# A convolution by transforms on one core: the first group of transformed weights made from one copy of the weights, the second copy loaded later, and the other groups cut anew

## The chip, the core and the metric

The kernel runs on one NeuronCore of a Trainium2 chip. The core has TensorE (matrix products, PE in the profile, with PEld for the loading of its stationary operand), VectorE (DVE), ScalarE (ACT), GpSimd (POOL) and SyncE (SP), which issues nearly all transfers, and 16 DMA engines. TensorE writes to eight banks of PSUM; DVE or ACT then copy ("cast") a bank into SBUF. The metric is device microseconds for one execution. The kernel before takes 269.83 us, the median of three runs (269.64 to 270.08).

## The reference

One image of 224 x 224 pixels with 96 channels is convolved with 7 x 7 taps from 96 to 96 channels. The reference does it by real Fourier transforms; only the product over channels mixes them. The convolution wraps round at the edges, since the transforms have the image's size.

```python
# x: (1, 224, 224, 96) bf16, w: (7, 7, 96, 96) bf16
wp = jnp.pad(w, ((0, H - K), (0, W - K), (0, 0), (0, 0)))
Xf = rfft2(x.astype(jnp.float32), axes=(1, 2))
Wf = rfft2(wp.astype(jnp.float32), axes=(0, 1))
Yf = jnp.einsum('bhwi,hwio->bhwo', Xf, Wf)
y = irfft2(Yf, s=(H, W), axes=(1, 2)).astype(jnp.bfloat16)
```

## The kernel before

The kernel does not transform the whole image. Down the image it takes eight blocks of 28 rows, each with a border of six, so 34 rows, and transforms these 34 rows into 17 real-pair "frequencies" (`NS = 17`; the first and the last, `REAL`, are two real numbers each, the other 15 a real and an imaginary part). Across the image it works on tiles of 32 pixels, seven of them (`NT = 7`), even and odd pixels being two planes, and treats the seven taps across by sums of shifted planes: 10 combinations of taps (`NTAP`, `TAPS`) in place of 14.

**The weights.** For each frequency the weights are needed transformed along the seven taps down, and combined along the seven taps across. The result is `WF` (96 input channels in partitions; 50 slots, 10 tap combinations, 96 output channels). A frequency has three slots: real part, imaginary part and their difference (two slots for frequency 0). WF is made on TensorE: the stationary operand is a strided view of the raw weights `wqx` (line 154; taps in partitions, 96 input channels by 96 output channels along each), the moving operand the selection matrix `Em` (line 157), which holds sine and cosine values times tap masks and lies behind the weights in the same buffer. The raw weights lie there twice: partition 2k + h holds tap k from output channel 48 h on, so that one product gives output channel o from the first copy and o + 48 from the second (half h of Em is zero in the partitions of the other). This is 98 partitions. Lines 182 to 187 load them in five chunks of columns, each as two transfers (tap 48 alone, then taps 0 to 47). Lines 188 and 189 let the second half of the first tile's pixels, `load_x(0, 1)`, wait for the third chunk.

`prep_jobs(gi)` (line 340) gives the jobs that make one group of frequencies. A job takes a bank, fills it with four products and has it cast to WF. The groups are `PGRP` (line 33). Group 0 (frequencies 0 and 1) is "full": all three slots come from products, 100 columns each, 12 jobs. The other five groups, three frequencies each, make two slots by products of 120 columns (12 jobs), and DVE subtracts one from the other for the third slot (`diff`, three jobs or two).

**The order of the work.** The calls are written in program order, and each engine runs its own in that order. At the start (lines 178 to 288) SP issues: the halo pixels (six pixels left of the first tile, two buffers `xh_bufs`), the first half of the first tile's pixels, the weight chunks, and the second half. All these pixel buffers lie in the last eight slots of WF, which are written late. TensorE runs 17 products of zeros (`warm`, line 195: filler), while DVE, ACT and POOL build the transform matrix `Fm` and Em from index arithmetic. Lines 699 to 717 then set TensorE's order: pixel transforms of the halos (`a_bank`) and of the first half (`f_jobs`, three parts by frequency, ten banks), 22 fillers, group 0 of the weights, the second half's first part, and then the planes `J` of the first three frequencies (`jit`, on DVE).

**The rounds.** `b_round(t, s)` (line 496) does one tile at one frequency: 33 products of WF with pixel planes in two banks (22 for a REAL frequency), sums on ACT, DVE and POOL, and every three frequencies a transfer to a scratch in DRAM. Frequency 0 of tile 0 is round 0. The first two tiles run interleaved, tile 1 four rounds behind (`LAG`). At two points of a round queued jobs may be run, counted by a slot number k: slots 2r and 2r + 1 belong to round r. A queue entry (a, b, jobs) runs its jobs evenly from slot a to slot b - 1 (`pace`, line 725). Lines 744 and 745 queue the weight groups so: group 1 in slots 0 and 1, group 2 in 4 to 8, and so on to slot 26. The rest of tile 0's pixel transforms and those of tiles 1 and 2 are queued there as well. The later tiles follow from line 808, with the inverse transforms (`c_jobs`), and a tail from line 846.

`evac` (line 120) decides whether DVE or ACT casts a bank: it adds up planned costs, 180 + n for DVE and 160 + 0.85 n for ACT with n columns, and takes the engine whose sum stays lower. The sums start at zero and are set anew before the rounds (line 721). When the last weight group is done, at round 15, the buffer of the raw weights is given back and later stages' pools open in its place (lines 778 to 788).

## Time and profile before

| what | value |
|---|---|
| median of three runs | 269.83 us |
| profiled execution: span from first to last instruction | 267.8 us |
| profiled execution: own time | the page gives its span alone; the median of the runs is 2.0 us above that span |
| PE busy | 258.4 us, 5144 products |
| DVE, ACT, POOL busy | 214.3, 194.6, 98.9 us |
| granted TensorE clock | 1.00 |
| moved by DMA | 46.78 MB, mean 175 GB/s |

The span is cut at the first and the last instruction, so it is a little shorter than the time of an execution. A group's line in the profile names the engine, the operation, what is written from what, the shapes and the count; in the timeline the first two numbers are the start and the length of a run of like instructions, in microseconds. In the table of stages each line has a stretch of time, its length, and then for PE, PEld, DVE, ACT and POOL the busy time and in brackets the number of instructions; at the end stand the granted clock, the DMA engines' busy share and the GB/s they moved. All work goes through helpers, so the source line of every instruction is that of one helper, and groups are told apart by tile names: wq is the buffer of the raw weights with Em, WF the transformed weights and also the early pixel buffers in it, xf the transformed pixels, J their planes, wu the zeros of the filler products, pb a PSUM bank.

### The profile page before, as it was taken

Reading aid. Unit: us, or ns where it says so; the run is one execution under the profiler, and the core shown is the slowest. Engines: PE = TensorE matmul, PEld = TensorE weight load, DVE = VectorE, ACT = ScalarE, POOL = GpSimd, SP = SyncE. Lnnn points to the kernel's source line nnn. Section 1 sums busy time; section 2 is a strip of 40 time slices with the busy share of each in tenths; the row PEclk is TensorE's granted clock in tenths of the full one; section 3 lists DMA queues with packets and bytes.
Section 4 is the critical chain, followed back from the end, with each engine's and each line's share of the span. In section 5 each row is a group of like instructions: output and inputs, shape, how many; then the busy total and the mean of one; then the engine's idle time right before and its main releaser. Section 6 shows DMA issues by size and latency. Waiting matters only on the chain. (4 is left out here: it accounts for less than half of the span.)

```text
span 267.8 us, 12172 instructions
## 1 busy us (share of the span) xinstructions
PE 258.4 (96%) x5144; PEld 237.3 (89%) x5144; DVE 214.3 (80%) x457; ACT 194.6 (73%) x483; POOL 98.9 (37%) x156
## 2 busy tenths in 40 slices
PE   8999999999999999999999999999999999999983
PEld 3679999999999999999999998999999889879862
DVE  5658998889899788779787888787898889878624
ACT  5558988587974577988988789887887854278113
POOL 7782315363656435321422222223222342532100
PEclk9999999999999999999999999999999999999999
DMA  6948011811111498997968487979777624887956
GB/s 169 233 130 213 11 47 46 239 48 72 47 47 50 146 266 143 281 272 199 299 170 241 116 221 235 238 204 329 269 148 216 202 98 154 198 229 186 257 115 206
DMA packets 47014, 46.78 MB, mean 175 GB/s; under 512 B 35286, under 2 KB 37986, under 8 KB 46960
## 3 DMA queue, kind: packets, MB, share of 16 engines
q1 hardware_dynamic: 44672, 43.94, 59.3%
q10 hardware_dynamic: 2288, 2.06, 2.6%
q8 instruction: 40, 0.66, 1.0%
q14 instruction: 14, 0.11, 0.2%
HBM read 24.65 MB, written 21.33 MB: 172 GB/s over the span
## 5 line engine op out<-in xcount | busy, mean ns | idle before, releaser
L89 PE MATMUL pb<-WF,J 96*128 96x96 bf16 x2821 | 162.8, 206 | 1.9 <-DVE J L89 1.1
L89 PEld LDWEIGHTS <-J 96*128 96x128 bf16 x2821 | 138.0, 98 | 12.4 <-issue 3.6
L89 POOL TENSOR_TENSOR yf<-v,u 128x384 bf16<-128x384 f32 x79 | 81.4, 1042 | 146.3 <-issue 84.6
L89 ACT CAST xf<-pb 96x408 bf16<-96x408 f32 (+3 forms) x145 | 67.7, 490 | 9.0 <-PE pb L89 5.4
L89 PE MATMUL pb<-WF,xf 96*128 96x96 bf16 x952 | 59.9, 206 | 0.5 <-ACT xf L89 0.5
L89 DVE TENSOR_TENSOR J<-xf 96x1824 bf16<-96x1824 bf16 (+1 forms) x84 | 56.9, 716 | 0.1
L89 PEld LDWEIGHTS <-xf 96*128 96x128 bf16 x952 | 47.0, 98 | 0.7 <-ACT xf L89 0.6
L89 PE MATMUL pb<-Fm,xn 118*128 118x136 bf16 (+3 forms) x640 | 45.5, 199 | 0.2 <-DVE u L89 0.2
L89 PE MATMUL pb<-tt,Gm 102*84 102x384 bf16 (+1 forms) x132 | 32.7, 326 | 0.4 <-ACT J L89 0.3
L89 ACT CAST WF<-pb 96x480 bf16<-96x480 f32 (+1 forms) x59 | 29.1, 578 | 4.8 <-PE pb L89 4.8
L89 PEld LDWEIGHTS <-xn 118*128 118x128 bf16 x640 | 30.3, 97 | 0.3 <-issue 0.3
L89 ACT CAST J<-pb 84x384 bf16<-84x384 f32 (+1 forms) x64 | 27.7, 490 | 2.6 <-PE pb L89 2.6
L89 ACT CAST yo<-pb 84x384 bf16<-84x384 f32 (+1 forms) x63 | 27.1, 486 | 2.3 <-POOL yf L89 1.3
L89 DVE TENSOR_TENSOR J<-J 96x912 bf16<-96x912 bf16 (+2 forms) x42 | 24.2, 577 | 0.0
L89 PE MATMUL pb<-wq 98*128 98x120 bf16 (+1 forms) x288 | 21.3, 226 | 0.0
L89 PEld LDWEIGHTS <-wq 98*128 98x128 bf16 x288 | 19.6, 151 | 0.2 <-issue 0.2
L89 PE MATMUL pb<-wu 128*128 128x512 bf16 (+1 forms) x75 | 16.8, 385 | 1.1 <-DVE ct L89 1.1
L89 PEld LDWEIGHTS <-wu 128*128 128x128 bf16 (+1 forms) x75 | 8.8, 120 | 8.0 <-issue 2.8
L89 DVE TENSOR_TENSOR yf<-v,u 128x384 bf16<-128x384 f32 x26 | 14.9, 572 | 0.9
L89 PEld LDWEIGHTS <-Gm 102*84 102x84 bf16 (+1 forms) x132 | 11.1, 117 | 1.0 <-issue 0.4
L89 ACT COPY xf<-xf 96x816 bf16<-96x816 bf16 (+3 forms) x20 | 11.3, 633 | 0.0
L89 DVE CAST WF<-pb 96x480 bf16<-96x480 f32 (+1 forms) x13 | 7.5, 609 | 4.2 <-PE pb L89 4.2
(386 smaller groups left out, 234.2 us busy)
## 6 DMA issues: line engine op xcount, KB each, us to landing
scr<-yf SPq DMA_DIRECT2D x30, 288.0 KB
xn<-in_x_dram SPq DMA_DIRECT2D x12, 672.0 KB
tt<-scr SPq DMA_DIRECT2D x24, 336.0 KB
out_dram<-yo SPq DMA_DIRECT2D x12, 252.0 KB
out_dram<-J SPq DMA_DIRECT2D x12, 252.0 KB
tt<-scr SPq DMA_DIRECT2D x6, 288.0 KB
WF<-in_x_dram SPq DMA_DIRECT2D x2, 672.0 KB
out_dram<-tt SPq DMA_DIRECT2D x8, 168.0 KB
```

The costliest lines, as they stand in the source:

```text
L89: r = fn(*a, **k)
```

## The change

The raw weights lie in another order: partition 49 h + k holds tap k from output channel 48 h on. So partitions 0 to 48 are one complete copy (all 96 x 96 columns), partitions 49 to 97 the second copy, shifted by 48 output channels. `load_w(h)` loads one copy in three transfers: tap 48 in two pieces of 16 short runs each, and taps 0 to 47 in one transfer of 48 rows. SP's order becomes: first half of the first tile's pixels, first copy, halos, second half of the pixels, second copy; the wait of the second half for a weight chunk is gone. Em starts 48 columns later, and its index arithmetic follows the new order: two operations more on DVE (`hf`, `tap`), four fewer on POOL, and POOL's clearing of the early pixel buffers' ends stands before the masks in place of behind them.

Group 0 is now four frequencies, made by `wide_jobs`: 24 jobs of four products each (96 products), over the 49 rows of the first copy with half 0 of Em, 110 columns, all slots at once. The other groups have 3, 3, 3 and 4 frequencies and still use both copies; the last one's banks hold 3 products of 160 columns, 16 jobs. Their slots are set by `PWIN`: 0 to 6, 7 to 11, 12 to 16 and 17 to 23.

TensorE's order at the start becomes: 16 fillers, the first half's pixel transforms, 4 fillers (`FILL`), 16 wide jobs (`WMID`), the halos, the second half's first part, the other 8 wide jobs. The raw weights' buffer is given back at round 14.

```diff
--- before.py
+++ after.py
@@ -25,12 +25,13 @@
 TW = 16
 HALO = 3
 PXC = 16
-NB = 8
+NB0 = 4
 POS = TW + HALO
 NTAP = 10
 TAPS = ((7, 8, 9, 6), (0, 2, 4, 6), (1, 3, 5))
 NSLOT = 2 + 3 * (NS - 1)
-PGRP = ((0, 2), (2, 5), (5, 8), (8, 11), (11, 14), (14, 17))
+PGRP = ((0, 4), (4, 7), (7, 10), (10, 13), (13, 17))
+PWIN = (None, (0, 7), (7, 12), (12, 17), (17, 24))
 YGRP = ((0, 3), (3, 6), (6, 9), (9, 12), (12, 15), (15, 17))
 YGRPL = ((0, 3), (3, 6), (6, 9), (9, 12), (12, 15), (15, 17))
 SA = 9
@@ -44,8 +45,8 @@
 MERGE = ()
 NP2 = 0
 WARM = 36
-NWC = 5
-HOLD = 2
+FILL = 4
+WMID = 16
 BIAS = 3000.0
 
 
@@ -152,9 +153,9 @@
     stmp_cm = tc.tile_pool(name="stmp", bufs=1)
     stmp = stmp_cm.__enter__()
     wqx = wtmp.tile([128, C - 1 + 127 * C + 1], BF16, name="wq")
-    wq = wqx[0:PW2]
     WC = C * C - C2
-    Em = wqx[0:PW2, WC:WC + 2 * NSLOT * NTAP].rearrange("p (h a t) -> p h a t", h=2, a=NSLOT)
+    WE = C * C
+    Em = wqx[0:PW2, WE:WE + 2 * NSLOT * NTAP].rearrange("p (h a t) -> p h a t", h=2, a=NSLOT)
     XHW = PAD * C + 32
     late = WF[0:R, NSLOT - 8:NSLOT].rearrange("p a t o -> p (a t o)")
     x0_bufs = [late[:, i * (XW + 32):(i + 1) * (XW + 32)] for i in range(2)]
@@ -176,17 +177,22 @@
         return load_rows(xbuf(t, jg), jg, t * 2 * TW, 2 * TW)
 
     wsrc = w.rearrange("kh kw i o -> (kh kw) (i o)")
+
+    def load_w(h):
+        n = (C * C, WC)[h]
+        off = wsrc.offset + h * C2
+        p = h * PW
+        m = n // 16
+        for a, b in ((0, m // 2), (m // 2, m)):
+            dma(wqx[p + PW - 1:p + PW, 0:n].rearrange("p (c m) -> p c m", c=16)[:, :, a:b],
+                bass.AP(wsrc.tensor, off + (PW - 1) * C * C + a, [[C * C, 1], [m, 16], [1, b - a]]))
+        dma(wqx[p:p + PW - 1, 0:n], bass.AP(wsrc.tensor, off, [[C * C, PW - 1], [1, n]]))
+    load_x(0, 0)
+    load_w(0)
     for jg in range(2):
         load_rows(xh_bufs[jg], jg, W - PAD, PAD)
-    load_x(0, 0)
-    wcut = [WC * c // NWC // 128 * 128 for c in range(NWC)] + [WC]
-    wdma = []
-    for c0, c1 in zip(wcut, wcut[1:]):
-        for k, n in ((PW - 1, 1), (0, PW - 1)):
-            wdma.append(dma(wqx[2 * k:2 * (k + n), c0:c1],
-                bass.AP(wsrc.tensor, wsrc.offset + k * C * C + c0, [[C * C, n], [C2, 2], [1, c1 - c0]])))
-    for d in load_x(0, 1):
-        tc.add_manual_dep(d.ins, wdma[2 * HOLD + 1].ins.name, SYNC, reason="second pixels behind the weights")
+    load_x(0, 1)
+    load_w(1)
 
     wu = cpool.tile([128, 128], BF16, name="wu")
     wur = wu[:].unsqueeze(1).to_broadcast([128, 4, 128])
@@ -197,7 +203,7 @@
         for _ in range(n):
             TE.matmul(pwu[:].rearrange("p (a b) -> p a b", a=4), lhsT=wu[:, 0:128], rhs=wur, start=True, stop=True)
     warm(8)
-    warm(9)
+    warm(8)
 
     ntmp = [0]
 
@@ -217,7 +223,7 @@
     VE.memset(pi_t[:], math.pi)
     dmy = ftile([128, 1])
     SE.activation(out=dmy[:], in_=pi_t[:], func=ACTF.Sin, bias=0.0, scale=0.0)
-    zw = wqx[0:PW2, WC + 2 * NSLOT * NTAP:]
+    zw = wqx[0:PW2, WE + 2 * NSLOT * NTAP:]
     SE.copy(out=zw, in_=wu[0:PW2, 0:1].to_broadcast(list(zw.shape)))
 
     nrj = ftile([R, JG]); pw_i = ftile([R, 1]); aa = ftile([R, NS, 2]); phf = ftile([R, NS, 2]); phe = ftile([R, NS, 2])
@@ -234,7 +240,10 @@
         eng.tensor_scalar(out=out_ap, in0=out_ap, scalar1=MAGIC, scalar2=MAGIC, op0=ALU.add, op1=ALU.subtract)
 
     VE.tensor_scalar(out=nrj[:], in0=nrj[:], scalar1=0.0, scalar2=float(LC - 1), op0=ALU.max, op1=ALU.min)
-    floor_div(VE, thp[:], pw_i[:], 2 * KT)
+    hf = ftile([R, 1]); tap = ftile([R, 1])
+    VE.tensor_single_scalar(out=hf[:], in_=pw_i[:], scalar=float(PW), op=ALU.is_ge)
+    VE.scalar_tensor_tensor(out=tap[:], in0=hf[:], scalar=-float(PW), in1=pw_i[:], op0=ALU.mult, op1=ALU.add)
+    floor_div(VE, thp[:], tap[:], KT)
     VE.memset(aa[:, 0, 1:2], float(LC))
     VE.memset(aa[:, NS - 1, :], 0.0)
     VE.memset(phf[:, 0:NS:NS - 1, 1:2], LC / 2.0)
@@ -253,21 +262,20 @@
     for r, n, v in ((0, 0, 1.0), (0, LC, -1.0), (1, 1, -1.0), (1, L - 1, 1.0)):
         o = mf[:, :, 2 * NS - 2 + r:2 * NS - 1 + r]
         GE.affine_select(out=o, in_=o, pattern=[[-B, JG], [0, 1]], compare_op=ALU.not_equal, fill=v, base=-n, channel_multiplier=1)
+    for xb in x0_bufs:
+        GE.memset(xb[:, XW:], 0.0)
+    for xb in xh_bufs:
+        GE.memset(xb[:, PAD * C:], 0.0)
     iota(twc[:], [[1, KT]])
-    pm = ftile([PW2, 1]); twp = ftile([PW2, 1]); hf = ftile([PW2, 1]); mk = ftile([PW2, NTAP]); mk2 = ftile([PW2, 2, NTAP])
-    th14 = ftile([PW2, 1])
-    GE.tensor_single_scalar(out=th14[:], in_=thp[0:PW2], scalar=-2.0 * KT, op=ALU.mult)
-    GE.tensor_tensor(out=pm[:], in0=th14[:], in1=pw_i[0:PW2], op=ALU.add)
-    floor_div(GE, twp[:], pm[:], 2)
-    GE.tensor_single_scalar(out=th14[:], in_=twp[:], scalar=-2.0, op=ALU.mult)
-    GE.tensor_tensor(out=hf[:], in0=th14[:], in1=pm[:], op=ALU.add)
+    twp = ftile([PW2, 1]); mk = ftile([PW2, NTAP]); mk2 = ftile([PW2, 2, NTAP])
+    th7 = ftile([PW2, 1])
+    GE.tensor_single_scalar(out=th7[:], in_=thp[0:PW2], scalar=-float(KT), op=ALU.mult)
+    GE.tensor_tensor(out=twp[:], in0=th7[:], in1=tap[0:PW2], op=ALU.add)
     GE.tensor_scalar(out=mk[:, 0:KT], in0=twc[:], scalar1=twp[:, 0:1], scalar2=None, op0=ALU.is_equal)
     GE.tensor_tensor(out=mk[:, KT:NTAP], in0=mk[:, 0:6:2], in1=mk[:, 1:6:2], op=ALU.add)
-    GE.tensor_scalar(out=mk2[:, 1], in0=mk[:], scalar1=hf[:, 0:1], scalar2=None, op0=ALU.mult)
+    GE.tensor_scalar(out=mk2[:, 1], in0=mk[:], scalar1=hf[0:PW2, 0:1], scalar2=None, op0=ALU.mult)
     GE.tensor_tensor(out=mk2[:, 0], in0=mk[:], in1=mk2[:, 1], op=ALU.subtract)
-    for xb in xh_bufs:
-        GE.memset(xb[:, PAD * C:], 0.0)
-    for xb in x0_bufs + xn_bufs:
+    for xb in xn_bufs:
         GE.memset(xb[:, XW:], 0.0)
     for xb in xf_bufs:
         GE.memset(xb[:, :, :, NS - 1, POS - 1, :].rearrange("c p r j -> c (p r) j"), 0.0)
@@ -337,31 +345,46 @@
 
     g_fin = build_g(3)
 
+    def wide_jobs():
+        n = slot(PGRP[0][1] - 1, 2) + 1
+        ncol = n * NTAP
+        assert NB0 * ncol <= 512 and C % NB0 == 0
+
+        def mk_(ob):
+            def f():
+                pw = bank()
+                pv_ = pw[:, 0:NB0 * ncol].rearrange("p (k q) -> p k q", q=ncol)
+                ev = Em[0:PW, 0, 0:n, :].rearrange("p a t -> p (a t)")
+                o0 = ob * NB0
+                for k in range(NB0):
+                    o = o0 + k
+                    TE.matmul(pv_[:, k], lhsT=wqx[0:PW, o:o + 127 * C + 1:C], rhs=ev, start=True, stop=True)
+                wv = WF[0:C, 0:n].rearrange("i a t o -> i (a t) o")
+                apart(("W", 0), ob, evac(wv[..., o0:o0 + NB0], pv_[0:C].rearrange("i k q -> i q k"), NB0 * ncol))
+            return f
+        return [mk_(ob) for ob in range(C // NB0)]
+
     def prep_jobs(gi):
         s0, s1 = PGRP[gi]
         ns = s1 - s0
-        full = gi == 0
-        ncol = (NSLOT_OF(s0, s1) if full else 2 * ns) * NTAP
+        ncol = 2 * ns * NTAP
+        hb = 256 // ncol
+        NB = 2 * hb
         nb = C // NB
-        hb = NB // 2
-        assert NB * ncol <= 512 and C2 % hb == 0
+        assert C2 % hb == 0
 
         def mk_(ob):
             def f():
                 pw = bank()
                 pv_ = pw[:, 0:NB * ncol].rearrange("p (k h q) -> p k h q", h=2, q=ncol)
                 ev = Em[:, :, slot(s0, 0):slot(s1 - 1, 2) + 1, :]
-                ev = ev.rearrange("p h a t -> p h (a t)") if full else ev.rearrange("p h (s r) t -> p h s (r t)", r=3)[:, :, :, 0:2 * NTAP]
+                ev = ev.rearrange("p h (s r) t -> p h s (r t)", r=3)[:, :, :, 0:2 * NTAP]
                 for k in range(hb):
                     o = ob * hb + k
                     TE.matmul(pv_[:, k], lhsT=wqx[0:PW2, o:o + 127 * C + 1:C], rhs=ev, start=True, stop=True)
                 pv_ = pv_[0:C]
                 o0, o1 = ob * hb, (ob + 1) * hb
                 wv = WF[0:C, slot(s0, 0):slot(s1 - 1, 2) + 1]
-                if full:
-                    wv = wv.rearrange("i a t (h o) -> i (a t) h o", h=2)
-                    apart(("W", gi), ob, evac(wv[..., o0:o1], pv_.rearrange("i k h q -> i q h k"), NB * ncol))
-                    return
                 wv = wv.rearrange("i (s r) t (h o) -> i s (r t) h o", r=3, h=2)
                 apart(("W", gi), ob, evac(wv[:, :, 0:2 * NTAP, :, o0:o1],
                       pv_.rearrange("i k h (s q) -> i s q h k", s=ns), NB * ncol))
@@ -373,10 +396,7 @@
                 w0, w1, w2 = (WF[0:C, slot(s, r)].rearrange("i t o -> i (t o)") for r in range(3))
                 VE.tensor_tensor(out=w2, in0=w0, in1=w1, op=ALU.subtract)
             return f
-        return [mk_(ob) for ob in range(nb)] + ([] if full else [diff(s) for s in range(s0, s1) if s not in REAL])
-
-    def NSLOT_OF(s0, s1):
-        return slot(s1 - 1, 2) + 1 - slot(s0, 0)
+        return [mk_(ob) for ob in range(nb)] + [diff(s) for s in range(s0, s1) if s not in REAL]
 
     xf_tiles = {}
 
@@ -697,18 +717,20 @@
         pump()
 
     xf0 = new_xf(0)
-    for jg in range(2):
-        for f in a_bank(0, xf0, xh_bufs[jg], 0, 3, jg, 0):
-            f()
     fj = [f_jobs(0, p) for p in range(3)]
     for p in range(3):
         for f in fj[p][0]:
             f()
-    for n in (11, 11):
-        warm(n)
-    for f in prep_jobs(0):
+    warm(FILL)
+    wide = wide_jobs()
+    for f in wide[:WMID]:
         f()
+    for jg in range(2):
+        for f in a_bank(0, xf0, xh_bufs[jg], 0, 3, jg, 0):
+            f()
     last = [f() for f in fj[0][1]]
+    for f in wide[WMID:]:
+        f()
     for jg in range(2):
         for d in load_x(1, jg):
             tc.add_manual_dep(d.ins, last[0].ins.name, SYNC, reason="second tile's pixels later")
@@ -742,7 +764,7 @@
         qs.append([a, b, jobs, len(jobs)])
 
     for gi in range(1, len(PGRP)):
-        add(2 * PGRP[gi - 1][0], 2 * PGRP[gi - 1][1] - (2 if gi == 1 else 1), prep_jobs(gi))
+        add(*PWIN[gi], prep_jobs(gi))
     for t in range(2):
         scr_tiles[t] = dr_pool.tile([TW, NJ, NS, 4 * C], BF16, name="scr")
     bursts = {}
```

## The prediction

> **What bounds the kernel now.** I read the page's shares of busy time first, then busy time by stage.
>
> ```profile
> PE 258.4 (96%) x5144; PEld 237.3 (89%) x5144; DVE 214.3 (80%) x457; ACT 194.6 (73%) x483; POOL 98.9 (37%) x156
> ```
> ```profile
> 10.96:15.71 4.75, 4.75 (x30) 2.19 (x26) 1.14 (x3) 0.58 (x1) 3.52 (x18) 1.00 0.97 255
> 15.71:20.23 4.52, 4.06 (x81) 3.94 (x80) 3.92 (x8) 3.76 (x8) 3.89 (x12) 1.00 0.19 54
> 20.23:35.67 15.44, 15.30 (x362) 15.16 (x363) 14.18 (x27) 14.62 (x36) 3.68 (x5) 1.00 0.43 116
> 80.00:236.00 156.00, 154.40 (x3174) 144.85 (x3172) 130.78 (x279) 119.74 (x308) 53.39 (x56) 1.00 0.73 202
> ```
> From 20.23 us on TensorE is the bound: 154.40 of 156 us busy between 80 and 236, 15.30 of 15.44 in the first rounds. There it is closely followed: DVE 14.18 and ACT 14.62 of 15.44. Before 20.23 a busy TensorE means little, as the order of its work shows:
>
> ```profile
> 1.05 5.83 PE L89 MATMUL pb<-wu 128*128 128x512 bf16 x17 [1.05 <-DVE ct L89]
> 7.62 3.49 PE L89 MATMUL pb<-Fm,WF 118*128 118x136 bf16 x103 [0.44 <-POOL WF L89]
> 10.96 4.91 PE L89 MATMUL pb<-wu 128*128 128x512 bf16 x22
> 15.71 3.13 PE L89 MATMUL pb<-wq 98*128 98x100 bf16 x48
> 18.68 1.10 PE L89 MATMUL pb<-Fm,WF 118*128 118x64 bf16 x32
> 20.23 0.51 PE L89 MATMUL pb<-WF,xf 96*128 96x96 bf16 x8 [0.46 <-ACT xf L89]
> 20.58 2.17 PE L89 MATMUL pb<-wq 98*128 98x120 bf16 x32
> 22.59 0.76 PE L89 MATMUL pb<-WF,J 96*128 96x96 bf16 x14
> 29.51 0.93 PE L89 MATMUL pb<-wq 98*128 98x120 bf16 x12
> ```
> The wu products are filler: 22 of them cover the wait for the weights. Round 0 starts at 20.23, and what follows is nearly all useful. So the time after is: when round 0 starts, plus what TensorE still has to do then. The casts that empty the banks, and the transfers, are the other views:
>
> ```profile
> 16.14 2.09 DVE L89 CAST WF<-pb 96x400 bf16<-96x400 f32 x4 [4.04 <-PE pb L89]
> 20.75 1.51 DVE L89 TENSOR_TENSOR J<-xf 96x1824 bf16<-96x1824 bf16 x2
> 16.40 2.78 ACT L89 CAST WF<-pb 96x400 bf16<-96x400 f32 x6 [4.61 <-PE pb L89]
> ```
> ```profile
> 3.11 7.20 SPq L89 DMA_DIRECT2D wq<-in_w_dram  x10
> 12.93 0.79 SPq L89 DMA_DIRECT2D WF<-in_x_dram  x2
> ```
> ```profile
> 5.00:6.00 1.00, 1.00 (x6) 0.41 (x5) 0.77 (x7) 0.00 (x0) 0.69 (x4) 1.00 1.02 294
> 8.00:9.00 1.00, 0.98 (x30) 0.83 (x28) 1.00 (x2) 0.81 (x2) 0.89 (x2) 1.00 1.02 229
> 12.00:13.00 1.00, 1.00 (x6) 0.49 (x5) 0.10 (x1) 0.00 (x0) 0.74 (x4) 1.00 1.04 246
> ```
>
> **The change part by part.** *Transfers.* In 1000-byte kB: one pixel load 118 x 6144 B = 725, a halo pair 272, first copy 49 x 18432 = 903, second 898. The GB/s of the one-microsecond windows (0, 21, 150, 187, 289, 294, 246, 226, 229, 240, 240, 248, 246 from 0 on) sum to 725 at 5.3 us, 1628 (pixels and first copy) at 8.9, 2625 (halos and second pixels too) at 13.0; at 245 GB/s on from there all 3523 have moved at 16.7. From moved to seen: SP waited until 12.93 for the third of five chunks, whose bytes (272 + 725 + 3/5 of 1797 = 2075) were through at 10.8, so 2.1 us. The first copy is then seen at 11.0, second pixels at 15.1, second copy at 18.8. The curve of before starts with short halo rows (150 and 187); with the pixels' 289 to 294 from 2 us on, all is 0.5 us sooner: 10.5. I take 10.8. SP's issuing is no limit: at 0.38 us a pixel load (2.26 for 6) and 0.72 a weight load, the first copy's three are out at 3.7 and the last at 8.2. Four issues fewer and the lost wait at 12.93 are worth nothing by themselves.
>
> *Constants.* POOL loses four small operations of its mask chain (about 1.1 us of 4.34 to 7.50) and does four memsets (0.31) before it: masks at 6.7 in place of 7.5. DVE gets two one-column operations (0.2 us each): Fm ready at 5.8 in place of 5.4, covered by the 16 filler products that end near 6.5. The selection matrix Em keeps its 1000 columns (1.4 us): 6.7 to 8.1, ahead of DVE's first pixel cast.
>
> *Start of TensorE.* First pixels, moved at 4.5 to 5.3, are seen between 6.6 and 7.4; 96 products at 32 ns (3.49 us for 103 wider ones) take 3.0; four fillers 0.86 (22 in 4.75). The wide group starts near 10.9, as the copy arrives.
>
> *Wide group, halos, second pixels.* 96 products, at 63 ns each (twelve from 29.51 to 30.27), are 6.05 us; with halos (0.7) and second pixels (1.1) 7.85. The trace has none with 49 rows: half of 63 is the lower end and 63 the upper, and I take 63; the casts decide either way. A cast of 400 columns cost DVE 0.523 (2.09/4) and ACT 0.463, single ones of 480 are 0.08 longer on either, so 440 cost 0.56 and 0.50. With four halo casts and four of 512 (DVE 0.53 and 0.62, ACT 0.47 and 0.53), all on DVE would be 18.0 us, all on ACT 15.9; the planner's costs give DVE 45%: 8.1 and 8.7 us. The slower queue decides: start 10.9, 0.43 to the first cast (15.71 to 16.14), 8.7 of casts, 0.1: round 0 at 20.1, against 20.23. If the casts were free, TensorE's 7.85 and 0.6 for the last bank would give 19.4; ten per cent dearer casts give 21.0. So fillers saved (19 x 0.216 = 4.1 us) go into making twice the frequencies, and the start moves by only -0.1.
>
> *Rounds.* TensorE has 240 weight products behind 20.23 before and 144 + 48 after: 48 x 63 = 3.04 less. The last group's 48 run 160 columns: 0.416 ns a column by the fillers (512 in 216, less a fixed 3) gives 69 against 63: +0.28. Net -2.76. There are 52 weight casts in place of 60 and 12 differences in place of 14: (8 x 0.57 + 2 x 0.60)/2 = 2.9 us less for the pair of engines. So the relief is nearly the same whether TensorE or the pair sets the pace. Round 0's fill falls from eight jobs to three (0.76 us); J's first operation (1.1 us) starts as DVE's last wide cast ends, near 19.5, done by 20.7 when it is wanted: no stall, and one of 0.5 at most if DVE runs late. The first fill needs the second copy at 20.5, seen at 18.8; each microsecond beyond that holds round 0's J products, queued behind it, by as much. Second pixels are wanted at 15.8 and seen at 15.1. From round 4 on the weight jobs are denser (37 in 17 slots, 36 in 20), but the pair's demand there, about 34 us, stays under TensorE's 37: nothing, +0.5 if it binds in places. The pools of the later stages open a round sooner, behind the last weight job: nothing. Second tile's loads, two microseconds sooner, run after the second copy: nothing.
>
> *Sum.* -0.1 - 2.76 = -2.9 us. The profiled span of 267.8 would be 264.9. The page gives no other time for that execution; the median of the runs, 269.83, is 2.0 above its span, which I carry over: **266.9 us**.
>
> **Rivals.**
>
> *First copy late (slower).* It lands in 49 partitions by rows of 18 KB, which this trace has nowhere: the time is 266.9 plus its delay behind 10.9, so no gain is left if it is seen at 13.8. Rates of a busy queue bound it: 294 GB/s (pixels), and 118 in the slice from 247 to 247.5 us with a DMA share of 1.01, where the tail's reloads go mostly into 64 partitions. At 118 it takes 7.7 us from 5.3, is seen at 15.1, and the time is 271.1. Against it: those reloads move pieces of 384 B, while long pixel rows got 289 to 294. [...]
>
> *The wide group waits for both copies (the change doesn't do what it says).* Both lie in one buffer; if the wait is kept for the whole buffer, the group starts at 18.8: 7.9 us later, 274.8. What speaks for it is that the kernel itself has to declare parts of a buffer independent for the casts (apart). Against it: pixel products ran at 7.62 while the other pixel buffer of the same WF was filled only after 12.93. [...]
>
> *Copy moderately late*, seen at 12.2 to 13.3: 268.2 to 269.3.
>
> *More than the sum.* The copy seen at 10.2 and casts 5% cheaper give -1.1, fewer stalls in the crowded first rounds up to -0.4: 265.4.
>
> **How the numbers follow.** The forecast, with its own range of 265.4 to 268.2 (start -0.8 to +1.3, rounds -0.7), has 0.70. Moderately late 0.11; no measurable change, 269.3 to 270.4 (seen 13.3 to 14.4), 0.05; later than that 0.08; the wait for both 0.06. This gives faster 0.81, same 0.05, slower 0.14, with 0.2% (0.54 us) as what a measurement here can tell from nothing. The range 265.4 to 269.3 holds 0.81.
>
> **What the profile after would show.** Wide products (49 rows, 110 columns) starting near 10.9 after four fillers, with little idle time and casts back to back on both engines until 20; second copy still arriving to 16.7. Round 0 (first product of WF with xf) near 20.1; 12 weight products and not 32 between it and the first J products; round 0 to round 4 shorter by about 2.3 us. Wrong if the 49-row products wait for DMA beyond 13.8, if round 0 starts past 22.9, or if TensorE idles over 2 us more between 20 and 80.

## The result

The kernel after takes 280.64 us (median of four runs, 278.67 to 284.09), the kernel before 269.95 beside it (269.64 to 270.12). The ratio of the two is 1.0376, with a 95% interval from 1.0308 to 1.0443: slower by 10.7 us, where 2.9 us less were forecast. The profiled execution took 278.85 us, with a span of 276.8 against 267.8. In the four runs the granted clock's mean was 0.975, 0.957, 0.954 and 0.975, and the two with the lower clock are the two long ones (282.44 and 284.09, of which the ratio leaves out the second).

The page's shares of busy time and the row of the granted clock, kernel after:

```profile
PE 259.8 (94%) x5125; PEld 241.2 (87%) x5125; DVE 217.4 (79%) x460; ACT 201.5 (73%) x484; POOL 97.7 (35%) x152
...
PEclk9957999997999999999999999999999999999999
```

There are 19 products fewer, yet PE's busy time rose by 1.4 us, and the clock's row, which was full before, has dips in slices 3 and 4 (13.8 to 27.7 us), and again in slice 10 (62 to 69). The order of TensorE's work in the kernel after:

```profile
6.31 2.69 PE L90 MATMUL pb<-Fm,WF 118*128 118x64 bf16 x96 [0.18 <-DMA WF<-in_x_dram]
8.84 1.02 PE L90 MATMUL pb<-wu 128*128 128x512 bf16 x4
12.76 5.33 PE L90 MATMUL pb<-wq 49*128 49x110 bf16 x64 [2.90 <-DMA wq<-in_w_dram]
18.02 3.22 PE L90 MATMUL pb<-Fm,WF 118*128 118x136 bf16 x44
21.18 2.15 PE L90 MATMUL pb<-wq 49*128 49x110 bf16 x32
24.06 0.50 PE L90 MATMUL pb<-WF,xf 96*128 96x96 bf16 x8 [0.73 <-ACT WF L90]
24.39 1.34 PE L90 MATMUL pb<-wq 98*128 98x120 bf16 x12
...
61.54 0.50 PE L90 MATMUL pb<-WF,xf 96*128 96x96 bf16 x8
63.83 0.47 PE L90 MATMUL pb<-WF,J 96*128 96x96 bf16 x7 [1.79 <-DVE J L90]
```

The first copy is seen at 12.76 after a wait of 2.90 us; round 0 begins at 24.06 and not at 20.1; at 62 TensorE waits 1.79 us for VectorE's planes. The casts of the wide group stood as priced on ACT (five in 2.49 us, 0.50 each). DVE's seven took 0.70 each and not 0.56, since they came at the pace of TensorE's half clock; at full clock (the kernel with 17 fillers and runs of 2, below) seven took 3.96 us, 0.57 each:

```profile
13.23 2.49 ACT L90 CAST WF<-pb 96x440 bf16<-96x440 f32 x5 [3.95 <-PE pb L90]
13.48 4.89 DVE L90 CAST WF<-pb 96x440 bf16<-96x440 f32 x7 [2.87 <-PE pb L90]
```

To see where the time came in, I line the traces up by the start of the same product of WF with xf (there are 952, eight to a round), and take its time after less its time before:

| product | before, us | after, us | difference |
|---|---|---|---|
| 0 (round 0) | 20.23 | 24.06 | +3.83 |
| 48 | 38.98 | 43.82 | +4.84 |
| 112 | 57.23 | 61.54 | +4.31 |
| 144 | 65.97 | 74.12 | +8.15 |
| 224 | 85.05 | 93.69 | +8.63 |
| 951 (last) | 250.38 | 259.07 | +8.69 |

So 3.83 us come in before round 0, about 0.5 from there to product 112, 4.3 between products 112 and 224 (where the last group of weights is made), and nothing behind. The stretches between those products in the table of stages (length, then busy time of PE, PEld, DVE, ACT and POOL), before:

```profile
20.23:57.23 37.00, 36.66 (x869) 36.38 (x869) 34.05 (x65) 30.61 (x76) 12.08 (x13) 1.00 0.38 105
57.23:85.05 27.82, 27.27 (x638) 26.98 (x636) 24.03 (x48) 21.09 (x51) 16.20 (x17) 1.00 0.15 56
20.23:85.05 64.82, 63.92 (x1502) 63.36 (x1503) 58.08 (x111) 51.70 (x125) 28.28 (x29) 1.00 0.28 84
```

and after; the last line lies 9 us behind 80 to 236 of the kernel before, and its shares are nearly the same (154.35 of 156 us for TensorE, where it had 154.40):

```profile
14.30:21.10 6.80, 6.80 (x86) 6.65 (x84) 5.38 (x9) 5.16 (x11) 4.58 (x13) 0.50 0.64 158
24.06:61.54 37.48, 36.95 (x854) 36.81 (x853) 32.02 (x59) 30.74 (x73) 11.91 (x11) 0.95 0.29 86
61.54:93.69 32.15, 27.59 (x606) 27.02 (x604) 25.59 (x50) 23.14 (x45) 15.61 (x16) 0.95 0.13 49
89.00:245.00 156.00, 154.35 (x3175) 144.84 (x3173) 129.18 (x276) 120.66 (x311) 53.20 (x55) 1.00 0.73 203
```

In the rounds TensorE's idle time (length less busy) went from 0.90 us to 5.08, and its busy time rose by 0.63 (from 63.92 to 36.95 + 27.59) although 48 weight products are gone from them. The granted clock stands at 0.50 from 14.3 to 21.1, 24.5 to 27.9 and 65.5 to 68.9: stretches of 3.4 us or two of them.

### The profile page after: what moved, and what is told of

It reads as the page before. It is cut to its first block, busy times and chain, and to the rows that moved or that the text cites. A ratio compares the mean times of both kernels' runs of the same rounds, so it can differ in the third digit from the quotient of the medians.

```text
span 276.8 us, 12123 instructions
## 1 busy us (share of the span) xinstructions
PE 259.8 (94%) x5125; PEld 241.2 (87%) x5125; DVE 217.4 (79%) x460; ACT 201.5 (73%) x484; POOL 97.7 (35%) x152
## 4 chain that ended last, share of the span: by engine, by line
PE 73%; DMA 10%; DVE 9%; ACT 4%; issue 2%; SPq 1%; ACTq 0%; DVEq 0%
PE pb L90 73%; DMA wq<-in_w_dram 3%; DVE J L90 3%; DMA xf<-scra 2%; DMA tt<-scr 2%; DVE v L90 2%; DVE WF L90 2%; ACT WF L90 2%; SPq L90 1%; DMA scrb<-yf 1%; DMA xf<-scrb 1%; DVE u L90 1%; ACT J L90 1%; DVE yf L90 1%; ACT xf L90 1%
## 5 line engine op out<-in xcount | busy, mean ns | idle before, releaser
L90 DVE TENSOR_TENSOR J<-xf 96x1824 bf16<-96x1824 bf16 (+1 forms) x84 | 56.2, 709 | 0.0
L90 ACT CAST WF<-pb 96x480 bf16<-96x480 f32 (+1 forms) x59 | 35.1, 666 | 6.8 <-PE pb L90 6.7
L90 PE MATMUL pb<-wq 98*128 98x120 bf16 (+2 forms) x288 | 24.9, 245 | 2.9 <-DMA wq<-in_w_dram 2.9
L90 PEld LDWEIGHTS <-wq 98*128 98x128 bf16 (+1 forms) x288 | 22.2, 152 | 3.4 <-issue 3.4
L90 DVE CAST WF<-pb 96x440 bf16<-96x440 f32 (+1 forms) x17 | 11.0, 657 | 3.6 <-PE pb L90 2.9
L90 PE MATMUL pb<-wu 128*112 128x384 bf16 (+1 forms) x56 | 12.1, 376 | 1.1 <-DVE ct L90 1.1
L90 PEld LDWEIGHTS <-wu 128*112 128x112 bf16 (+1 forms) x56 | 6.8, 124 | 5.5 <-issue 2.2
```

Of the source, the lines that this page charges most:

```text
L90: r = fn(*a, **k)
```

## The experiments

Six theories were tested. **A**: idle time ahead of the wide group halves the clock. **B**: the last group's casts, whose innermost runs in WF are three elements long instead of four, are dear. **C**: the first copy is late since its partitions are only part of all. **D**: a group's differences, three in a row on VectorE ahead of the planes J, make TensorE wait. **E**: products over 49 rows leave TensorE too little active, and this halves the clock. **F**: VectorE is as full as TensorE in the rounds, so that fewer products alone bring little.

**Fillers up to the copy (A).** `FILL` goes from 4 to 17; in a second kernel the last group also takes two products a bank (runs of 2), and a third has that group's change alone.

```diff
-FILL = 4
+FILL = 17
```

> The changed kernel with 17 fillers in place of 4 between the first pixels and the first copy (13 more of 0.216 us, 2.8 us, so TensorE has work while it waits). Theory A (TensorE's idle 2.9 us before the first copy halved its clock from 14.3 to 21.1 us and, after the next gap, from 24.5 to 27.9): no half clock before 60 us, the first copy still seen near 12.7, round 0 at 12.8 + 0.43 + 8.7 + 0.1 = 22.0 in place of 24.06, time 3 to 4 us below the changed kernel, 275 to 277. The loss between 57 and 87 us stays. Rival (the casts set that stage's pace, the clock doesn't matter): round 0 stays near 24, time within 0.5 us of the changed kernel.

277.72 us, ratio 1.0256 (1.0219 to 1.0293). In its profile TensorE has no gap ahead of the wide group, and yet the clock is halved for 13.7 us:

```profile
9.72 3.83 PE L90 MATMUL pb<-wu 128*128 128x512 bf16 x17
13.49 4.56 PE L90 MATMUL pb<-wq 49*128 49x110 bf16 x64
```
```profile
16.70:30.40 13.70, 13.09 (x161) 12.73 (x160) 8.32 (x14) 10.17 (x23) 3.03 (x8) 0.50 0.49 133
```

So a gap is not needed, and A as stated falls, although the time fell by about the 3 us that A forecast (by the two ratios 3.2). The mean clock was 0.969 in this profile and 0.980 to 0.988 in the other three executions, so none ran at full clock throughout.

```diff
-        hb = 256 // ncol
+        hb = min(256 // ncol, 4 if ns == 3 else 2)
```

> The changed kernel with the last group's banks holding 2 products of 160 columns (24 casts of 320 columns, runs of 2 output channels) in place of 3 (16 casts of 480, runs of 3). Theory B (a cast that writes runs of three 2-byte values costs 0.9 us on ScalarE and 1.2 on VectorE, and these 16 casts hold up TensorE from 57 to 87 us): casts of 320 at 0.38 to 0.48, the distance to the kernel before grows by less than 1.5 us between 57 and 87 us in place of 4.5, time 3 to 4 us below the changed kernel. Rival (the slots 17 to 23 are crowded, whatever the runs): 24 jobs in place of 16 make it no better, 0 to +1 us.

279.3 us, ratio 1.0343 (1.0308 to 1.0377), not to be told from the kernel after: the 3 to 4 us that B forecast did not come. The last group's casts of 320 columns in runs of 2 took 565 ns on ACT, about as much as a cast of 480 in runs of 4. There are more of them, so this route saves nothing and says nothing on B.

> Both edits. If theories A and B are both right and add: 6 to 8 us below the changed kernel, 270 to 273, that is within 1.2% of the kernel before; what stays is the start of round 0 at about 22.0 in place of 20.23. If only one of the two is a cause: 275 to 277.

276.95 us, ratio 1.0193 (1.0123 to 1.0263). Here the start of the profiled execution drew half clock only from 22.2 to 25.6:

```profile
13.26 4.16 PE L90 MATMUL pb<-wq 49*128 49x110 bf16 x64
17.35 1.82 PE L90 MATMUL pb<-Fm,WF 118*128 118x136 bf16 x44
19.10 2.13 PE L90 MATMUL pb<-wq 49*128 49x110 bf16 x32
21.96 0.60 PE L90 MATMUL pb<-WF,xf 96*128 96x96 bf16 x8 [0.72 <-ACT WF L90]
```

At full clock the 44 pixel products take 1.82 us and not 3.22, and round 0 begins at 21.96, 8.7 us behind the first wide product, where the kernel after needs 11.3. The start of this kernel is that of the one with 17 fillers alone; how much half clock an execution draws there differs from run to run.

**Runs of 3 in the kernel before (B).**

```diff
-NB = 8
...
+        NB = 6 if gi == len(PGRP) - 1 else 8
```

> The kernel before with one thing changed: its last weight group fills a bank with 3 products of 120 columns (16 casts of 360 columns, runs of 3) in place of 4 (12 casts of 480, runs of 4). Theory B: these casts cost 0.7 us (ScalarE) to 0.95 (VectorE) in place of some 0.46 to 0.51 for 360 columns, and the kernel is 0.5 to 2.5 us slower. Rival (runs of 3 cost nothing of their own): 4 casts more, 0.6 us for two engines, within 0.3 us.

273.25 us (273.05 to 273.37), ratio 1.0106 (1.0083 to 1.0129): 2.9 us more, and not 0.5 to 2.5, from 16 casts of 360 columns in place of 12 of 480. The two traces agree up to 66 us. The casts of weights between 57 and 90 us, in this kernel and then in the kernel after:

```profile
L88 ACT CAST WF<-pb 96x360 bf16<-96x360 f32 x16 | 10.7, 808 | 0.0
L88 ACT CAST WF<-pb 96x480 bf16<-96x480 f32 x8 | 4.0, 574 | 0.0
```
```profile
L90 ACT CAST WF<-pb 96x480 bf16<-96x480 f32 x18 | 14.7, 931 | 0.0
L90 DVE CAST WF<-pb 96x480 bf16<-96x480 f32 x1 | 1.2, 1210 | 0.0
```

A quarter fewer columns cost 808 ns and not 574: B is confirmed. (The mean of 931 mixes three casts in runs of four with fifteen in runs of three; the fifteen alone took 1.00 us on average, 0.90 to 1.25.) Why a run of three costs so much more than one of four no run here shows.

**The copies exchanged; the copy in four chunks (C).**

```diff
-    load_w(0)
+    load_w(1)
...
-    load_w(1)
+    load_w(0)
```

> The changed kernel with the two copies' loads exchanged: the second copy (898 kB, partitions 49 to 97) is loaded behind the first pixels, the first copy (903 kB, partitions 0 to 48) last. The wide group then waits for the late one, so the time is worse; what is measured is when the copy that is loaded first is seen, by SyncE's wait for it. Theory C (what limits a copy is the half of the partitions that it lands in): the copy in partitions 49 to 97, which lie on both sides of 64, moves faster than 134 GB/s and is seen 1 to 2 us sooner, 10.7 to 11.7 in place of 12.7. Rival (18 kB rows, or the copy's place in the queue): seen at 12.5 to 12.9 as before.

One run, 289.49 us, since the wide group now waits for the copy that is loaded last. The trace's transfers show the copy in partitions 49 to 97 moving from 4.16 to 8.89 us (898 kB, 190 GB/s), where the first copy, in 0 to 48, took from 4.41 to 11.15 (903 kB, 134 GB/s). SP's last weight issue, which waits for the earlier copy, shows the same: it ends at 11.21 here, at 13.77 in the kernel after (start and length of SP's runs, this kernel and then the kernel after).

```profile
6.72 4.49 SPq L90 DMA_DIRECT2D wq<-in_w_dram  x3
```
```profile
7.04 6.73 SPq L90 DMA_DIRECT2D wq<-in_w_dram  x3
```

```diff
-        dma(wqx[p:p + PW - 1, 0:n], bass.AP(wsrc.tensor, off, [[C * C, PW - 1], [1, n]]))
+        for a, b in zip(range(0, n, n // 4), range(n // 4, n + 1, n // 4)):
+            dma(wqx[p:p + PW - 1, a:b], bass.AP(wsrc.tensor, off + a, [[C * C, PW - 1], [1, b - a]]))
```

> The changed kernel with each copy's main transfer cut into four by columns (rows of 4608 B in place of 18432 B), the same partitions. Theory C (the partitions): first copy seen at 12.4 to 13.2, no sooner than the changed kernel's 12.7. Rival (long rows move slowly): seen at 10.5 to 11.2, as 240 GB/s would have it, and round 0 about 2 us sooner.

One run, 280.8 us. With rows a quarter as long the copy is seen at 12.48, only 0.28 sooner. So the length of the rows is not the cause. The stages (DMA share and GB/s at the end) while it moves:

```profile
7.00:8.00 1.00, 0.88 (x31) 0.91 (x32) 0.98 (x2) 0.45 (x1) 0.91 (x2) 1.00 1.08 152
8.00:9.00 1.00, 1.00 (x46) 1.00 (x42) 1.00 (x2) 1.00 (x4) 0.71 (x4) 1.00 1.04 157
9.00:10.00 1.00, 1.00 (x35) 0.84 (x31) 1.00 (x4) 0.77 (x2) 0.71 (x4) 1.00 1.02 147
```

The DMA engines are full at 147 to 157 GB/s, about half of the 294 that the pixels got into 118 partitions. C holds for these two copies: in the same place of the queue 134 GB/s into partitions 0 to 48 and 190 into 49 to 97. That the border lies at 64, as the expectation has it, no run shows.

**The differences apart (D).** Each difference gets a slot of its own ahead of the round that uses it, and the casts' windows (`PWIN`) start and end a slot sooner, on top of fillers and runs of 2; a second kernel keeps runs of 3.

```diff
     for gi in range(1, len(PGRP)):
-        add(*PWIN[gi], prep_jobs(gi))
+        add(*PWIN[gi], prep_jobs(gi)[:-3])
+    later = []
+    for gi in range(1, len(PGRP)):
+        for s, f in zip(range(*PGRP[gi]), prep_jobs(gi)[-3:]):
+            later.append((dslot[s], f))
...
+    for k, f in later:
+        add(k, k + 1, [f])
```

> The kernel with 17 fillers and runs of 2, with one more edit: the twelve differences (diff, on VectorE) no longer stand in threes behind a group's casts but one to a slot, between the slots in which the planes J are made; the cast jobs' windows start and end a slot sooner. Theory D (three differences of 0.88 us in a row ahead of J keep TensorE waiting 1.8 us near 60 us and 0.7 + 0.9 near 81, and its clock is halved for 3.4 us after each): these three gaps and both half-clock stretches vanish, 5 to 7 us below the run with 17 fillers and runs of 2 (275.0 span), that is a span of 268 to 270 and a time within 1% of the kernel before. Rival (the casts of runs of 2, 12.4 us on ScalarE, hold it up): the gaps move but their sum stays, within 1.5 us.

276.83 us, ratio 1.0254 (1.022 to 1.0289). In VectorE's order of the kernel after, three differences stand ahead of the planes that TensorE waits for at 62:

```profile
60.13 2.63 DVE L90 TENSOR_TENSOR WF<-WF 96x960 bf16<-96x960 bf16 x3
62.69 0.54 DVE L90 SCALAR_TENSOR_TENSOR v<-tt__1637,pb 128x384 f32<-128x384 f32 x1
63.15 0.62 DVE L90 TENSOR_TENSOR J<-J 96x912 bf16<-96x912 bf16 x1
```

Spread, this wait and the half-clock stretches of the rounds are gone; TensorE's longest wait there is 0.93 us. From product 112 to 224 the kernel loses 0.85 us against the kernel before, where the one with fillers and runs of 2 alone loses 4.65. The median is the same all the same, because the start drew more half clock here: from 16.4 to 30.0 us in the profile (mean clock 0.971, as in two of the other three runs), where the other kernel's profile (0.981) had 3.4 us of it. So D names the wait rightly, and its remedy works where it is applied; the start hides it in the medians. It has a price: the eight differences between 57 and 95 us cost 1243 ns each instead of the 935 of the kernel after.

> The same with the last group's 16 casts of 480 columns in runs of 3, as in the changed kernel. 16 casts at 0.88 on ScalarE against 24 at 0.56 are 14.1 against 13.4 us: within 1.5 us of the run with runs of 2 if theory D holds; 2 to 4 us slower if runs of 3 are a cause of their own (theory B).

276.91 us, ratio 1.0252 (1.0218 to 1.0285): the same median as with runs of 2. From product 112 to 224 its profile loses 3.28 us and not 0.85, but the two kernels' clocks differed from run to run (means 0.971 to 0.984 and 0.973 to 0.994, where the profile has the 0.973), so that the pair settles nothing.

> The kernel before with its differences spread one to a slot, as in the changed kernel's version with spread differences; groups, casts and loads stay. Theory D on the kernel before: its waits for J (0.3 near 32, 0.6 near 58, 0.5 near 87 us; 1.4 in all) shrink to half or less, 0.5 to 1.2 us faster. Rival (they wait for VectorE's whole load, not for the bunching): within 0.4 us.

The same spreading put into the kernel before gave 271.32 us, ratio 1.0074 (1.0058 to 1.0091): 1.8 us slower, which neither side had forecast. The differences between 20.2 and 105.3 us, before and then spread:

```profile
L89 DVE TENSOR_TENSOR WF<-WF 96x960 bf16<-96x960 bf16 x14 | 9.3, 711 | 0.4 <-ACT WF L89 0.4
```
```profile
L89 DVE TENSOR_TENSOR WF<-WF 96x960 bf16<-96x960 bf16 x14 | 14.0, 1003 | 1.7 <-ACT WF L89 1.6
```

Spreading makes them dearer by 0.3 us each, and the traces show why. A difference that meets no sum of GpSimd (`yf` from `v` and `u`) takes 0.64 to 0.66 us. One that begins while such a sum runs (for over 0.1 us more) ends 0.51 to 0.52 us after the sum does, so it takes up to 1.5 us: all 92 such cases in the sixteen traces agree. In the kernel before 4 of the 14 differences began within a sum, spread 8 of 14; between 57 and 95 us it was 3 of 6 in the kernel after and all eight in the kernel with spread differences.

**49 rows against 98 (E).** Both kernels load both copies ahead of the halos and the second pixels, with 38 fillers, the whole wide group in one piece, and the spreading with runs of 2. The only difference of the two is that one takes the wide products over 49 rows and the other over 98, with zeros in the moving operand for the second copy.

```diff
-FILL = 4
-WMID = 16
+FILL = 38
+WMID = 24
...
-                ev = Em[0:PW, 0, 0:n, :].rearrange("p a t -> p (a t)")
+                ev = Em[:, 0, 0:n, :].rearrange("p a t -> p (a t)")
...
-                    TE.matmul(pv_[:, k], lhsT=wqx[0:PW, o:o + 127 * C + 1:C], rhs=ev, start=True, stop=True)
+                    TE.matmul(pv_[:, k], lhsT=wqx[0:PW2, o:o + 127 * C + 1:C], rhs=ev, start=True, stop=True)
```

> For the clock alone, one of a pair: both copies are loaded before halos and second pixels, 38 fillers bridge to about 17.5 us, and all 24 wide jobs run in one go, over the 49 rows of the first copy. TensorE has no gap before them. Theory E (what halves the clock is not idle time alone: the 49-row products paced by casts keep too little of the array busy): half clock within 17 to 30 us, in most of the runs, and a mean granted clock below 0.99. Rival (only gaps of 1.8 us and more do it): clock 1.00 until 60 us.

> The pair's other half: the same kernel, but the wide products run over 98 rows (both copies; the moving operand is zero in the second copy's rows, so the sums are the same). Theory E: no half clock there, or in fewer runs, and round 0 sooner by 0.5 to 2 us than with 49 rows. Rival: no difference between the two.

49 rows: 280.6 us (280.13 to 280.87), ratio 1.0406 (1.039 to 1.0423). 98 rows: 276.62 us (276.23 to 276.64), ratio 1.0257 (1.0242 to 1.0272). TensorE's order and a stage of the first, then of the second:

```profile
17.74 6.50 PE L90 MATMUL pb<-wq 49*128 49x110 bf16 x96
24.17 3.25 PE L90 MATMUL pb<-Fm,WF 118*128 118x136 bf16 x44
```
```profile
23.00:33.20 10.20, 9.95 (x126) 9.40 (x125) 6.05 (x11) 7.66 (x17) 1.02 (x1) 0.50 0.52 139
```
```profile
17.98 6.08 PE L90 MATMUL pb<-wq 98*128 98x110 bf16 x96
23.90 1.81 PE L90 MATMUL pb<-Fm,WF 118*128 118x136 bf16 x44
```
```profile
23.00:33.20 10.20, 9.12 (x207) 8.87 (x206) 7.61 (x16) 9.34 (x24) 1.03 (x1) 1.00 0.54 145
```

With 49 rows the clock is halved from 23.0 to 33.2, behind 8.4 us of fillers without a gap; with 98 rows it stays full to the end. E's forecast holds, for 4.0 us; how much of TensorE was active no run measures, so that this is the cause stays a theory. The other profiles agree: all nine of kernels with 49-row products show half clock before 60 us, 3.4 to 23.9 us of it (five of them had no wait ahead of these products; mean clocks 0.945 to 0.982), and the three of kernels with 98 rows (two follow below; mean clocks 0.994 to 1.00) show none before 60 us.

This kernel of 98 rows also shows the rounds at full clock (from product 112 to 224, then from round 0 to 224):

```profile
63.24:91.90 28.66, 26.04 (x600) 25.25 (x598) 28.26 (x51) 18.61 (x48) 15.70 (x16) 1.00 0.14 54
26.20:91.90 65.70, 62.16 (x1454) 61.09 (x1455) 60.04 (x111) 50.68 (x124) 27.92 (x27) 1.00 0.27 83
```

TensorE's busy time in the rounds is 1.76 us less than before (63.92), so the products' relief is there. Its idle time is 3.54 us and not 0.90, 3.1 of it waits for VectorE's J, and VectorE has 60.04 us of work where it had 58.08. In the first line VectorE is the bound, busy for 28.26 of 28.66 us (24.03 of 27.82 before); 4.05 us of its growth there are the differences, 7.65 in place of 3.60. In all the rounds take 0.88 us longer than before.

**Fewer products alone (F).** In the kernel before, each bank of the later groups gets one product of 480 columns in place of four of 120. Casts, differences and everything else are as they were. Three of four products are left out, so WF and the output hold other numbers.

```diff
+                if not full:
+                    o = ob * hb
+                    fv_ = Em.rearrange("p h a t -> p (h a t)")[:, 0:NB * ncol]
+                    TE.matmul(pw[:, 0:NB * ncol], lhsT=wqx[0:PW2, o:o + 127 * C + 1:C], rhs=fv_, start=True, stop=True)
-                for k in range(hb):
+                for k in range(hb if full else 0):
```

> The kernel before with TensorE's load in the rounds made lighter and nothing else: in the five later weight groups a bank is filled by one product of 480 columns (near 0.20 us) in place of four of 120 (0.25). The other products are left out, so WF holds other numbers; casts, differences, sums and planes stay. TensorE loses 60 x 0.05 = 3.0 us of work. The prediction's reading (TensorE is the bound in the rounds, and lighter products shorten it one for one): 2.5 to 3.2 us faster. Theory F (VectorE is as full, so the time goes into TensorE's waits for J): 0 to 1.2 us faster, and TensorE's waits for J grow by about as much as it lost in work.

268.76 us (ten runs), ratio 0.9967 (0.9952 to 0.9982): 0.7 us less. The weight products of the later groups, before and in this kernel:

```profile
L89 PE MATMUL pb<-wq 98*128 98x120 bf16 x240 | 18.1, 226 | 0.0
```
```profile
L89 PE MATMUL pb<-wq 98*128 98x480 bf16 x60 | 15.5, 370 | 0.1
```

In the profile TensorE's busy time from round 0 to product 224 fell by 1.95 us (63.92 to 61.97), its idle time rose from 0.90 to 1.65, and the stretch is 1.20 shorter. So F holds in part: of the 1.95 us that TensorE is spared, 1.20 are gained in the profile's rounds and 0.7 in the medians, even with no work added elsewhere.

**The changed kernel's own rounds at full clock; its last group cut 3 and 1 (B and D again).** The first has the start with 98 rows and the changed kernel's groups, windows, runs of 3 and differences in a row. The second cuts the last group into frequencies 13 to 15 (runs of 4) and 16 alone, which takes 48 products more.

```diff
-PGRP = ((0, 4), (4, 7), (7, 10), (10, 13), (13, 17))
-PWIN = (None, (0, 7), (7, 12), (12, 17), (17, 24))
+PGRP = ((0, 4), (4, 7), (7, 10), (10, 13), (13, 16), (16, 17))
+PWIN = (None, (0, 7), (7, 12), (12, 17), (17, 24), (24, 28))
```

> The start of the run with 98-row wide products (its clock stayed at 1.00), and the changed kernel's own rounds behind it: runs of 3 in the last group, differences in threes, its windows. So the rounds are seen without half clock. If the half clock was only a follower of the start, the distance to the kernel before, 6.0 us at round 0, stays within 1 us up to 90 us. If the new cut of the groups costs by itself (runs of 3, differences next to J): it grows by 2 to 4 us between 57 and 87 us, and the waits of 1.8 and 1.4 us are there at full clock; each may then halve the clock for one stretch of 3.4.

> The same with the last group cut into frequencies 13 to 15 (12 casts of 480 columns in runs of 4) and 16 alone (4 casts in runs of 12; 48 products of 40 columns more, some 2 to 3 us of TensorE). Theory B (runs of 3 are most of that loss): the growth between 57 and 87 us falls by 1.5 to 3 us although TensorE has more to do. Rival (the windows and the differences are the loss): within 1 us, or worse by the added products.

282.08 us, ratio 1.0442 (1.0408 to 1.0477), and 279.52 us, ratio 1.0348 (1.0313 to 1.0383). The first is at +6.22 us at round 0 and at +6.08 at product 112, all at full clock, and at +11.76 at product 224: it loses 5.7 us there, with 3.4 us of half clock (89.0 to 92.5):

```profile
63.31:96.81 33.50, 28.27 (x605) 27.26 (x603) 25.14 (x50) 23.06 (x45) 15.60 (x16) 0.95 0.12 46
```

In the second, whose last groups have runs of 4 and 12, the growth is 3.8 us (from +5.88 to +9.70), in spite of the 48 products, and the casts between 57 and 95 us tell why (first kernel, second kernel; six of the first's 21 are in runs of four):

```profile
L90 ACT CAST WF<-pb 96x480 bf16<-96x480 f32 x21 | 16.1, 886 | 0.0
```
```profile
L90 ACT CAST WF<-pb 96x480 bf16<-96x480 f32 x21 | 10.7, 559 | 0.9 <-PE pb L90 0.9
```

TensorE's wait near 65 us is the same in both, so it does not come from these casts but from the differences in a row (D). Half clock follows it in the second (66.4 to 69.8), not in the first:

```profile
65.58 0.47 PE L90 MATMUL pb<-WF,J 96*128 96x96 bf16 x7 [1.76 <-DVE J L90]
```
```profile
65.33 0.47 PE L90 MATMUL pb<-WF,J 96*128 96x96 bf16 x7 [1.72 <-DVE J L90]
```

The first of these kernels and the one of 98 rows above (276.62 us) differ in three things alone: the differences in a row or spread, the windows a slot sooner, and runs of 3 or of 2. Together these are worth 5.5 us, with neither having half clock at the start. What each kernel's profile loses against the kernel before, by the products of WF with xf:

| kernel | runs of the last group | differences | product 112 to 144, us | 112 to 224, us |
|---|---|---|---|---|
| after | 3 | in a row | 3.84 | 4.32 |
| fillers, runs of 2 | 2 | in a row | 3.84 | 4.65 |
| 98 rows, own rounds | 3 | in a row | 3.49 | 5.68 |
| 98 rows, last group cut 3 and 1 | 4 and 12 | in a row | 3.27 | 3.82 |
| fillers, spread | 2 | spread | 0.48 | 0.85 |
| 98 rows, spread | 2 | spread | 0.47 | 0.84 |

The loss up to product 144 goes with the differences in a row (and the windows that were moved with them), whatever the runs. What is left in the last kernel is its start, 5.97 us late at round 0, and 0.88 in the rounds.

None of the versions that do the whole computation beats the kernel before.

## Why the prediction was wrong

*Transfers.* The first copy was to be seen at 10.8 to 10.9 and was seen at 12.76. The step that failed is pricing its bytes by the curve of a kernel whose weights lie in 98 partitions (229 to 248 GB/s); into partitions 0 to 48 the rate is 134 GB/s. The prediction had this as its rival "copy moderately late" (seen at 12.2 to 13.3), and by its reckoning it is worth 1.9 us. In the run with the copies exchanged the second copy, into partitions 49 to 97, moved at 190, a ratio of 1.42; what in the chip makes the two rates no run shows. SP's issues of the first copy were out at 3.5 us (3.7 forecast), and the first pixels were seen at 6.3, sooner than the 6.6 to 7.4 forecast. SP's last issue waited for the first copy and ended at 13.77 and not at 8.2, so the second copy moved until 19.65 and not 16.7; neither it nor the second pixels held TensorE up. The rival in which the group waits for both copies did not come.

*Wide group.* The sum from the copy to round 0 was 9.2 us. At full clock it takes 8.7, so the casts and their sharing were priced well, 0.5 too high. In the kernel after it takes 11.3: half clock, which the prediction's sum did not have. The kernel after has the wait of 2.90 us ahead of it; but in the kernel with 17 fillers the clock also fell with no gap of even a microsecond (13.7 us of half clock), and in the pair of 49 and 98 rows the rows in use made the difference (10.2 us against none). The prediction bounded the 49-row product between half of 63 ns and 63 by itself, and not by what it does to the products behind it. In the kernel after that wait and the 49 rows come together, and no run separates their shares there. Round 0 at 24.06 lies past the 22.9 that the prediction named as a sign that it is wrong.

*Rounds.* The term of -2.76 us failed. Its count was right (192 products for 240), and in the kernel of 98 rows with spread differences a TensorE at full clock had 1.76 us less to do; 160 columns cost 77 ns a product (nine in 0.69 us from 60.08) and not 69, which is 0.4 of the missing 1.0, and I can't place the rest. None of the 1.76 was gained: TensorE's idle time grew by 2.6 us at the same time. The sentence that failed is that the relief is the same whether TensorE or the pair sets the pace. The pair's own relief, 2.9 us for each engine, did not come: in the kernel after VectorE was busy for 57.61 us from round 0 to product 224 (58.08 before) and ScalarE for 53.88 (51.70 before). And the waits are nearly all for VectorE's J, at the few points where several jobs stand ahead of it, which no sum of work shows. Fewer products without any other edit gained 0.7 us. From 20 to 80 us TensorE idled for 4.5 us and not 1.1, the prediction's other sign of being wrong.

*Last group.* "Denser jobs: nothing, +0.5 if it binds in places" was the most expensive line: 4.3 us between products 112 and 224. It left out two things. A cast of the last group was taken to cost what others of 480 columns cost (0.57 us); in runs of 3 it took 0.81 us for 360 columns and 1.00 for 480 on ACT. In the kernel before such casts alone are worth 2.9 us, in the start with 98 rows some 2.6 (in spite of more products). And three differences in a row hold up J: 3.84 of the 4.3 us come by product 144, in the stretch with the wait of 1.8 us and the half clock from 65.5, and that loss is 0.5 in the kernels with spread differences, earlier windows and runs of 2. The two overlap and don't add up; how they share the 4.3 us was not separated.

*Sum.* Start +3.83 and rounds +4.81 (0.63 busy, 4.18 idle) make 8.6 of the 9.0 us between the two spans. The remaining 1.7 us between the medians go with the two executions whose clock was lower than the profiled one's (0.957 and 0.954 against 0.975).

## What to carry to other kernels

Price a transfer by a row that goes into the same partitions, and a cast by a row with the same innermost run; a byte or a column count alone was wrong by a factor of nearly 1.8 in both here. When a change thins out one engine's work, look for who waits for whom at the crowded spots: VectorE, at 90% of TensorE's load, held TensorE up where three of its jobs came in a row. Before you move such jobs apart, look at what runs beside them in the new place. And ask of every changed matrix product not only how long it takes but what it does to the granted clock of what comes next.

## What the runs showed of the hardware

- The granted clock halved without idle time ahead of it where products ran over 49 rows: 110 columns, 68 ns each (6.50 us for 96), 10.2 us of half clock and 4.0 us of time, against no half clock with 98 rows (6.08 us for 96). Executions of one kernel differ in how much of it they draw: mean clocks of 0.954 to 0.975 in the kernel after, 0.969 to 0.988 with 17 fillers.
- It also fell behind TensorE's wait of 1.7 to 1.8 us for J: 1.7 us after the wait's end in the kernel after (63.83, half clock from 65.5) and 1.1 with the last group cut 3 and 1 (65.33, from 66.4), but not in the kernel of 98 rows with its own rounds (65.58). Half clock came in stretches of 3.4 us or near a multiple of it: 3.4, 6.8, 10.2 and 13.7 us.
- A cast from PSUM to bf16 whose innermost runs are three elements long took 0.81 us for 360 columns and 1.00 for 480 on ScalarE, and 1.2 for 480 on VectorE (one cast); with runs of four, 0.57 to 0.59 and 0.64 for 480.
- A copy into partitions 0 to 48 moved at 134 GB/s, one into 49 to 97 at 190, and full columns of pixels into 118 partitions at 289 to 294.
- A difference of 960 columns on VectorE (bf16, both operands in SBUF) took 0.64 to 0.66 us beside no sum of GpSimd, and ended 0.51 to 0.52 us after the sum when it began within one. Their mean was 0.71 us in the kernel before and 1.00 there when spread over the rounds, 0.94 in the crowded stretch of the kernel after and 1.24 when spread there.
